# A decode attention block on one core: engines synchronized by hand, a TensorE loop, and a softmax that subtracts the maximum

## The chip, the cores and the metric

The kernel runs on one core of a Trainium2 chip. The metric is the device time of one execution in microseconds (us), the median of several runs. One profiled execution gives the trace; its page and its views are what is quoted below.

## The reference

Two sequences, one new token each (B = 2), model width D = 512. A is attention with a cache, B a small MLP block whose result gates it.

```python
xn = layernorm(x)                                  # (2, 1, 512)
# A: 32 query heads, 8 key/value heads, 32768 cached positions of width 128
q = xn @ wq                                        # (2, 32 heads, 1, 128)
scores = einsum(q, k) * 128 ** -0.5                # k, v: (2, 8, 32768, 128), each for 4 heads
s = (softmax(scores) @ v).reshape(2, 1, 4096) @ wo
# B: the shifted part is zero for a sequence of length 1
h2 = gelu(layernorm(xn) @ w3) @ w4
out = x + s * silu(xn + h2)
```

Nearly all the data is the cache: 16 pairs of K and V (2 sequences x 8 heads), each K and each V 32768 x 128 in bf16, 8.39 MB.

## The kernel before

The kernel is written against a tile framework, which allocates buffers from pools and puts in every semaphore. The work on the 16 head groups is written out, so each engine's program is one straight line.

Two rings in SBUF hold the cache: `kbuf` with three slots of 4.19 MB, `vbuf` with two. A K or V of one group takes two slots. Each partition holds 256 positions; a slot is one half of them (KPT = 128). All large loads are issued on SP's queue, in program order (lines 86, 95, 101, 114, 115, 392).

For each group `m`:

- `emit_k` is called twice, once per half. VectorE transposes K in 32x32 blocks (line 303), eight tiles `T` of 128x1024 per half, from a pool of four. TensorE multiplies each tile by the query, four matmuls of 512 columns with weights `z` (line 311), into one PSUM bank `sc`. ScalarE takes the exponential with the row sums `rs` (line 320), without subtracting a maximum. VectorE transposes the result into `pt` (line 322).
- Between the two calls the next K is issued: its slots come free when the first half of this one is transposed.
- `emit_v` is called for both halves. The row sums are added up over partitions with a matmul (line 339, `S`), and 32 matmuls per half multiply `pt` with V into the bank `o` (line 343). At the end `o` is copied (line 352), gathered (`oT`, line 355), divided by the sum (lines 360, 362) and spread (lines 365 to 372) into `oX`.
- After that the next V is issued: `vbuf` is free when the last of these matmuls is done.

Ahead of the groups stand the layernorms, the queries (line 215), and the MLP `emit_mlp`, whose weights lie in `vbuf`. Eight small loads of `x` and `xn` go through GpSimd (lines 109, 188). At the last group but one, `wo` is loaded behind the last V, in three parts, into the slot that is free by then; behind the last group 128 matmuls multiply `oX` with it (line 400), and two VectorE steps and two small stores make the output.

Of the kernel before, what the change touches and what calls it, by code (L numbers as in the profile page):

```python
# [9 lines left out]
BF16 = mybir.dt.bfloat16  # L10
ACT = mybir.ActivationFunctionType
ALU = mybir.AluOpType
AX = mybir.AxisListType

I32 = mybir.dt.int32

KPT = 128
# [4 lines left out]
EPS = 1e-5  # L22


@with_exitstack
def kernel(
# [35 lines left out]
    QP = 32 * (NQ - 1) + B  # L62

    pers = ctx.enter_context(tc.tile_pool(name="pers", bufs=1))
    rings = ctx.enter_context(tc.tile_pool(name="rings", bufs=1))
    ktp = ctx.enter_context(tc.tile_pool(name="ktp", bufs=T_BUFS))
    epp = ctx.enter_context(tc.tile_pool(name="epp", bufs=2))
    ptp = ctx.enter_context(tc.tile_pool(name="ptp", bufs=3))
    obp = ctx.enter_context(tc.tile_pool(name="obp", bufs=2))
    smp = ctx.enter_context(tc.tile_pool(name="smp", bufs=4))  # L70
    pro_ps = ctx.enter_context(tc.tile_pool(name="pro_ps", bufs=1, space=bass.MemoryType.PSUM))
    f_ps = ctx.enter_context(tc.tile_pool(name="f_ps", bufs=3, space=bass.MemoryType.PSUM))
    sc_ps = ctx.enter_context(tc.tile_pool(name="sc_ps", bufs=2, space=bass.MemoryType.PSUM))
    o_ps = ctx.enter_context(tc.tile_pool(name="o_ps", bufs=2, space=bass.MemoryType.PSUM))

    kbuf = rings.tile([128, 3 * SLOT], BF16, name="kbuf")
    vbuf = rings.tile([128, 2 * SLOT], BF16, name="vbuf")

    def row_view(cache, b, g):
        return cache[b, g, :, :].rearrange("(p t) d -> p (t d)", p=128)  # L80

    def load_k(b, g, base, parts=1):
        w = NPART * SLOT // parts
        src = row_view(A_k_cache, b, g)
        for c in range(parts):
            nc.sync.dma_start(
                out=kbuf[:, base * SLOT + c * w:base * SLOT + (c + 1) * w],
                in_=src[:, c * w:(c + 1) * w],
            )

    def load_v(b, g, parts=1):
        w = NPART * SLOT // parts
        src = row_view(A_v_cache, b, g)
        for c in range(parts):
            nc.sync.dma_start(out=vbuf[:, c * w:(c + 1) * w], in_=src[:, c * w:(c + 1) * w])  # L95


    x_bf = pers.tile([B, D], BF16)
    nc.scalar.dma_start(out=x_bf[:, :], in_=A_x[:, 0, :])
    wq_t = kbuf[:, 2 * SLOT:3 * SLOT]  # L100
    nc.sync.dma_start(  # L101
        out=wq_t[:, 0:DK * HD],
        in_=A_wq.rearrange("(p k) f -> p (k f)", k=DK),
    )

    x4_bf = pers.tile([128, QW], BF16)
    nc.gpsimd.memset(x4_bf[:, :], 0.0)
    for n in range(NQ):
        nc.gpsimd.dma_start(out=x4_bf[32 * n:32 * n + B, :], in_=A_x[:, 0, n * QW:(n + 1) * QW])
    groups = [(b, g) for b in range(B) for g in range(Hkv)]  # L110
    NG = len(groups)
    w34 = vbuf[:, 0:SLOT]
    W4O = DK * Fdim
    nc.sync.dma_start(out=w34[:, 0:W4O], in_=B_w3.rearrange("(p k) f -> p (k f)", k=DK))  # L114
    nc.sync.dma_start(out=w34[:, W4O:W4O + FK * D], in_=B_w4.rearrange("(p f) d -> p (f d)", f=FK))  # L115
    load_k(*groups[0], 0)


    ident = pers.tile([128, 128], BF16)
    make_identity(nc, ident[:, :])  # L120
    ones_f = pers.tile([128, 128], F32)
    nc.gpsimd.memset(ones_f[:, :], 1.0)


    sel = pers.tile([128, NB, 2, 4, 32], BF16)
    for j in range(4):
        nc.vector.tensor_copy(
            out=sel[:, :, :, j, :],
            in_=ident[:, :].rearrange("p (b w e) -> p b e w", b=NB, e=2),
        )  # L130

    sel_o = pers.tile([128, VT, rep], F32)
    nc.vector.tensor_reduce(
        out=sel_o[:, :, :],
        in_=ident[:, :].rearrange("p (j a t h) -> p a t h j", j=4, t=VT, h=rep)[:, 0, :, :, :],
        axis=AX.X, op=ALU.add,
    )
    sel_h = pers.tile([128, rep], F32)
    nc.vector.tensor_reduce(
        out=sel_h[:, :],  # L140
        in_=ident[:, :].rearrange("p (r h) -> p h r", h=rep),
        axis=AX.X, op=ALU.add,
    )

    sel_r = pers.tile([128, NQ, 4, 32], BF16)
    for j in range(4):
        nc.vector.tensor_copy(
            out=sel_r[:, :, j, :],
            in_=ident[:, :].rearrange("p (w r) -> p r w", r=NQ),
        )  # L150

    mask = pers.tile([128, NQ, rep], F32)
    for r in range(NQ):
        nc.vector.tensor_reduce(
            out=mask[:, r, :],
            in_=ident[:, :].rearrange("p (h w) -> p h w", h=rep),
            axis=AX.X, op=ALU.add,
        )

    zs = [pers.tile([128, NB, 2, ZC], BF16, name=f"z{i}") for i in range(2)]  # L160
    for z in zs:
        nc.gpsimd.memset(z[:, :, :, :], 0.0)


    xf = pers.tile([B, D], F32)
    nc.vector.tensor_copy(out=xf[:, :], in_=x_bf[:, :])

    def layernorm(dst, src, t):
        stats = pers.tile([B, nc.vector.BN_STATS_DIM], F32, name=f"stats_{t}")
        nc.vector.bn_stats(out=stats[:, :], in_=src[:, :])  # L170
        mv = pers.tile([B, nc.vector.BN_AGGR_DIM], F32, name=f"mv_{t}")
        nc.vector.bn_aggr(out=mv[:, :], in_=stats[:, :])
        rstd = pers.tile([B, 1], F32, name=f"rstd_{t}")
        nc.vector.tensor_scalar_add(out=rstd[:, :], in0=mv[:, 1:2], scalar1=EPS)
        nc.scalar.activation(out=rstd[:, :], in_=rstd[:, :], func=ACT.Sqrt)
        nc.vector.reciprocal(out=rstd[:, :], in_=rstd[:, :])
        nc.vector.tensor_scalar(
            out=dst[:, :], in0=src[:, :],
            scalar1=mv[:, 0:1], scalar2=rstd[:, 0:1],
            op0=ALU.subtract, op1=ALU.mult,  # L180
        )

    xn = pers.tile([B, D], F32)
    layernorm(xn, xf, "ln1")
    xn4 = pers.tile([128, QW], F32)
    nc.gpsimd.memset(xn4[:, :], 0.0)
    for n in range(NQ):
        nc.gpsimd.dma_start(out=xn4[32 * n:32 * n + B, :], in_=xn[:, n * QW:(n + 1) * QW])
    ln2 = pers.tile([B, D], F32)
    layernorm(ln2, xn, "ln2")  # L190
    xn_bf = pers.tile([B, D], BF16)
    nc.vector.tensor_copy(out=xn_bf[:, :], in_=xn[:, :])
    ln2_bf = pers.tile([B, D], BF16)
    nc.vector.tensor_copy(out=ln2_bf[:, :], in_=ln2[:, :])

    treg = pro_ps.tile([128, 2 * DK * B], BF16, tag="pro")
    for s, src in enumerate((xn_bf, ln2_bf)):
        for k in range(DK):
            c = (s * DK + k) * B
            nc.tensor.transpose(out=treg[:, c:c + B], in_=src[0:B, k::DK], identity=ident[0:B, 0:B])  # L200
    xT = pers.tile([128, 2 * DK, B], BF16)
    nc.vector.tensor_copy(out=xT[:, :, :], in_=treg[:, :].rearrange("p (k b) -> p k b", b=B))

    q_sb = pers.tile([128, B, Hq], BF16)

    oX = pers.tile([128, Hkv, NQ, B], BF16)
    g4 = pers.tile([128, QW], F32)
    x4 = pers.tile([128, QW], F32)
    nc.gpsimd.tensor_copy(out=x4[:, :], in_=x4_bf[:, :])

    wq3 = wq_t[:, 0:DK * HD].rearrange("p (k f) -> p k f", k=DK)
    qT_ps = pro_ps.tile([128, Hq * B], F32, tag="pro")
    for h in range(Hq):
        for k in range(DK):
            nc.tensor.matmul(  # L215
                qT_ps[:, h * B:(h + 1) * B],
                lhsT=wq3[:, k, h * Dh:(h + 1) * Dh],
                rhs=xT[:, k, :],
                start=(k == 0), stop=(k == DK - 1),
            )  # L220
    nc.vector.tensor_copy(out=q_sb[:, :, :], in_=qT_ps[:, :].rearrange("p (h b) -> p b h", b=B))

    qr_ps = pro_ps.tile([128, NB, 2, B * Hq], F32, tag="pro")
    for nb in range(NB):
        for e in range(2):
            nc.tensor.matmul(
                qr_ps[:, nb, e, :],
                lhsT=sel[:, nb, e, :, :].rearrange("p j w -> p (j w)"),
                rhs=q_sb[:, :, :].rearrange("p b h -> p (b h)"),
                start=True, stop=True,  # L230
            )
    qr = pers.tile([128, NB, 2, B, Hq], BF16)
    nc.vector.tensor_copy(  # L233
        out=qr[:, :, :, :, :].rearrange("p n e b h -> p (n e b h)"),
        in_=qr_ps[:, :, :, :].rearrange("p n e c -> p (n e c)"),
    )

# [54 lines left out]
    def emit_k(m, h, first):  # L292
        b, g = groups[m]
        if first:
            state["z"] = emit_z(b, g)
# [150 lines left out]
```

## Time and profile before

| what | value |
|---|---|
| time, median of 3 runs | 660.84 us (660.67 to 661.22) |
| span of the profiled execution, first to last instruction | 658.9 us |
| what lies around the span, median less span | 1.9 us |
| bytes read from HBM | 280.50 MB, 426 GB/s over the span |
| busy: PE, PEld, DVE, ACT, POOL | 386.7, 172.1, 346.0, 50.3, 6.9 us |
| mean granted TensorE clock | 0.825 |
| transposes of K, line 303 | 256, 1205 ns each |
| score matmuls, line 311 | 992 recorded, 421 ns each |

The profiled execution has no time of its own listed beside the timed runs; its span is compared with their median. PE is TensorE's matmuls, PEld its weight loads, DVE VectorE, ACT ScalarE, POOL GpSimd; SPq is SP's queue of transfers. "Landing" is the moment at which all parts of a transfer have been signalled. In the list of DMA queues the columns are packets, MB, and the share of the 16 DMA engines' time. The trace also holds every single DMA packet with its start, duration, size and queue.

### The profile page before, as it was taken

The numbers are of one execution on the slowest core, as the hardware profiler recorded it, in microseconds if no ns is written. First come the engines' busy times: TensorE is split into PE (matmuls) and PEld (weight loads), VectorE is DVE, ScalarE is ACT, GpSimd is POOL, SyncE is SP. The second block draws the span as 40 slices with busy tenths as digits, with TensorE's granted clock in tenths as the row PEclk, the third lists the DMA queues.
The fourth block names the chain that finished last, engine by engine and source line by source line (L and its number), as shares of the span: only waits on it lengthen the run. The fifth ranks groups of instructions, "written<-read, shape, count | busy, mean of one in ns | idle before, by whom it ended". The sixth has DMA issues, their size and how long they took to land.

```text
span 658.9 us, 6323 instructions
## 1 busy us (share of the span) xinstructions
PE 386.7 (59%) x2652; PEld 172.1 (26%) x2684; DVE 346.0 (53%) x442; ACT 50.3 (8%) x152; POOL 6.9 (1%) x20
## 2 busy tenths in 40 slices
PE   2338194673828557283764729377482946738764
PEld 2313132231313223131331313123131322313322
DVE  5147192754809265381935629183572918447560
ACT  1301001010100101000010100101010010100000
POOL 4000000000000000000000000000000000000000
PEclk9999688786968968697886959878596877859896
DMA  9999999999999999999999999999999999999995
GB/s 367 451 426 442 435 446 439 410 443 426 439 438 435 430 435 422 447 434 423 442 427 442 438 419 434 443 434 443 414 423 446 443 442 443 410 427 428 431 421 224
DMA packets 6704, 280.91 MB, mean 426 GB/s; under 512 B 906, under 2 KB 916, under 8 KB 1940
## 3 DMA queue, kind: packets, MB, share of 16 engines
q1 hardware_dynamic: 6408, 280.50, 98.6%
q8 instruction: 21, 0.34, 0.2%
q0 software_dynamic: 256, 0.01, 0.0%
q14 instruction: 7, 0.06, 0.0%
q10 hardware_dynamic: 12, 0.00, 0.0%
HBM read 280.50 MB, written 0.00 MB: 426 GB/s over the span
## 4 chain that ended last, share of the span: by engine, by line
DMA 75%; DVE 14%; issue 7%; PE 3%; SPq 0%; ACT 0%; DVEq 0%
DMA kbuf<-in_A_k_cache_dram 69%; DVE T L303 14%; DMA kbuf<-in_A_wo_dram 6%; PE sc L311 2%; PE o L343 1%; PE s_ps L400 0%; ACT ep L320 0%; SPq L95 0%; DVE pt L322 0%; SPq L115 0%; SPq L392 0%; SPq L114 0%; SPq L101 0%; PE S L339 0%; DVE sg L408 0%
## 5 line engine op out<-in xcount | busy, mean ns | idle before, releaser
L311 PE MATMUL sc<-T,z 128*128 128x512 bf16 x992 | 276.4, 421 | 206.3 <-DVE T L303 197.8
L303 DVE STREAM_TRANSPOSE T<-kbuf 128x1024 int32<-128x1024 int32 x256 | 291.5, 1205 | 150.5 <-DMA kbuf<-in_A_k_cache_dram 150.5
L311 PEld LDWEIGHTS <-z 128*128 128x128 bf16 x1024 | 105.7, 103 | 371.2 <-issue 278.7
L343 PE MATMUL o<-vbuf,pt 128*16 128x512 bf16 x1024 | 69.9, 434 | 3.2 <-DMA vbuf<-in_A_v_cache_dram 3.2
L320 ACT ACTIVATE ep<-sc 128x512 bf16<-128x512 f32 x32 | 19.1, 597 | 493.2 <-PE sc L311 451.2
L334 DVE MEMSET o<- 128x512 f32 x16 | 7.8, 485 | 69.3 <-ACT ob L352 68.3
L322 DVE STREAM_TRANSPOSE pt<-ep 128x512 bf16<-128x512 bf16 x32 | 22.6, 707 | 34.7 <-ACT ep L320 34.4
L343 PEld LDWEIGHTS <-pt 128*16 128x16 bf16 x1024 | 27.2, 99 | 37.9 <-issue 18.2
L339 PE MATMUL S<-sm,ones_f 128*128 128x4 f32 x64 | 10.7, 238 | 26.1 <-DVE sm L338 26.1
L355 PE MATMUL oT<-sel_o,ob 128*128 128x4 f32 x128 | 16.9, 255 | 11.1 <-ACT ob L352 11.1
L355 PEld LDWEIGHTS oT<-sel_o,ob 128*128 128x128 f32 x128 | 15.5, 191 | 19.3 <-ACT ob L352 19.3
L339 PEld LDWEIGHTS S<-sm,ones_f 128*128 128x128 f32 x64 | 10.7, 188 | 30.9 <-DVE sm L338 28.4
L352 ACT COPY ob<-o 128x512 f32<-128x512 f32 x16 | 9.4, 586 | 83.4 <-PE o L343 83.4
L362 DVE TENSOR_TENSOR on<-oT,rec 128x4 bf16<-128x4 f32 x16 | 2.6, 162 | 21.8 <-PE oT L355 21.8
L286 ACT COPY z<-qr 32x16 bf16<-32x16 bf16 x64 | 12.6, 198 | 11.5 <-DVE qr L233 10.9
L360 DVE RECIPROCAL rec<-S 128x4 f32<-128x4 f32 x16 | 2.9, 182 | 7.6 <-PE S L339 7.6
L365 PEld LDWEIGHTS <-sel_r 128*128 128x128 bf16 x64 | 5.2, 117 | 5.2 <-issue 5.2
L320 ACT ACTIVATION_READ_ACCUMULATOR ep<-sc 128x1 f32 x32 | 6.3, 198 | 0.2
L215 PE MATMUL qT_ps<-xT,kbuf 128*128 128x2 bf16 x128 | 3.6, 165 | 4.5 <-DMA kbuf<-in_A_wq_dram 4.5
L365 PE MATMUL xp<-on,sel_r 128*128 128x4 bf16 x64 | 3.8, 164 | 4.1 <-DVE on L362 4.1
L338 DVE TENSOR_SCALAR sm<-sel_h,rs 128x4 f32<-128x4 f32 x32 | 6.0, 188 | 0.0
L370 DVE TENSOR_TENSOR xm<-xp,mask 128x16 f32<-128x16 f32 x16 | 2.8, 174 | 5.3 <-PE xp L365 5.3
(64 smaller groups left out, 48.5 us busy)
## 6 DMA issues: line engine op xcount, KB each, us to landing
kbuf<-in_A_k_cache_dram SPq DMA_DIRECT2D x2, 4096.0 KB, 29.1
vbuf<-in_A_v_cache_dram SPq DMA_DIRECT2D x2, 4096.0 KB, 26.7
kbuf<-in_A_wq_dram SPq DMA_DIRECT2D x1, 4096.0 KB
vbuf<-in_B_w_dram SPq DMA_DIRECT2D x2, 1792.0 KB, 21.6
kbuf<-in_A_wo_dram SPq DMA_DIRECT2D x1, 2048.0 KB, 35.9
kbuf<-in_A_wo_dram SPq DMA_DIRECT2D x1, 1536.0 KB, 39.1
kbuf<-in_A_wo_dram SPq DMA_DIRECT2D x1, 512.0 KB
kbuf<-in_A_k_cache_dram SPq DMA_DIRECT2D x15, 29.4
```

Source lines behind the costliest of these rows:

```text
L286: nc.scalar.copy(out=z[32 * j:32 * j + 32, :, :, c:c + rep], in_=qr[32 * j:32 * j + 32, :, :, b, g * rep:(g + 1) * rep],)
L303: nc.vector.transpose(out=T[:, :].rearrange("p (b t k) -> p t b k", b=NB, t=RT), in_=kt[:, r * W:(r + 1) * W].rearrange("p (t b k) -> p t ...
L311: nc.tensor.matmul(sc[:, :], lhsT=z[:, nb, e, zc:zc + 128], rhs=Tb[:, nb, :, e], start=(r == 0 and nb == 0 and e == 0), stop=(r == NR - 1 ...
L320: nc.scalar.activation(out=ep[:, :], in_=sc[:, :], func=ACT.Exp, scale=inv_sqrt_dh, accum_out=rs[:, :])
L322: nc.vector.transpose(out=pt[:, :, :].rearrange("p r (t h) -> p t r h", h=rep), in_=ep[:, :].rearrange("p (t r h) -> p t r h", r=NR, h=rep),)
L334: nc.vector.memset(state["o"][:, :], 0.0)
L338: nc.vector.tensor_scalar_mul(out=sm[:, :], in0=sel_h[:, :], scalar1=rs[:, 0:1])
L339: nc.tensor.matmul(S[:, :], lhsT=ones_f[:, :], rhs=sm[:, :], start=(i == 0), stop=(i == NPART - 1))
L343: nc.tensor.matmul(o[32 * j:32 * j + VT * rep, :], lhsT=pt[:, r, a * VT * rep:(a + 1) * VT * rep], rhs=vt[:, u * VT:(u + 1) * VT, :].rearr ...
L352: nc.scalar.copy(out=ob[:, :], in_=o[:, :])
L355: nc.tensor.matmul(oT[:, :], lhsT=ob[:, t * Dh:(t + 1) * Dh], rhs=sel_o[:, t, :], start=(t == 0), stop=(t == VT - 1),)
L365: nc.tensor.matmul(xp[:, r, :], lhsT=sel_r[:, r, :, :].rearrange("p j w -> p (j w)"), rhs=on[:, :], start=True, stop=True,)
```

## The change

The computation is written in one section in which the framework puts in no semaphores. A small class `Queue` wraps each engine, counts the instructions that signal, and attaches the waits that are named by hand. Buffers are allocated once, by name.

- TensorE's work on a group is the body of a loop of 16 passes, whose first instruction lies at the start of a block of 256 instructions (`head_slot`). Its waits are on semaphores that it counts down again (`take`). The other engines' programs stay written out.
- The scores keep two banks; both exponentials of a group wait for the head's maximum over all positions: VectorE reduces each half (`peak`), a matmul with `same_h` spreads the row maxima, VectorE reduces again, and ScalarE subtracts the result in the exponential. `z` is one buffer instead of two, filled for the next group behind the exponentials.
- The next K now waits for the matmuls of the eighth tile (`s_T`) and not for its transpose; the next V waits for the last V matmul as before (`s_X`).
- The first half in `order(m)` no longer decides which V half comes first: it is always half 0.
- `o` is cleared once, not once per group. The MLP's second product is 14 matmuls of 512 columns instead of 56 of 128. The four small loads of `x` and four that spread the gate are issued on ScalarE's queue; GpSimd issues none.
- TensorE's built program shrinks from 344,320 to 65,152 bytes (64 bytes an instruction; the loop body has 317 instructions), VectorE's from 42,496 to 35,840.

The core of the changed side:

```diff
+    with tc.tile_critical(no_gpsimd_drain=True):
...
+        for n in range(NQ):
+            ac.op(lambda e, n=n: e.dma_start(out=x4_bf[32 * n:32 * n + B, :], in_=A_x[:, 0, n * QW:(n + 1) * QW]), e_x4z, inc=(d_x4, 16))
...
+        load_v(0, e_h2)
+        for m in range(1, NG):
+            half = (s_T, NT * (m - 1) + NR)
+            base = m % 2
+            if m < NG - 1:
+                sp.op(lambda e, m=m, base=base: e.dma_start(
+                    out=kbuf[:, base * SLOT:(base + NPART) * SLOT], in_=row_view(A_k_cache, *groups[m])),
+                    half, e_q, inc=(d_k[0], 16))
...
+            load_v(m, (s_X, NX * (m - 1) + 3))
...
+            def peak(i):
+                e = ve.op(lambda v: v.tensor_reduce(out=mx[:, i:i + 1], in_=sc[i][:, :], axis=AX.X, op=ALU.max), (s_T, m * NT + (i + 1) * NR))
+                ve.op(lambda v: v.tensor_scalar_mul(out=mxr[:, i, :], in0=row_of[:, :], scalar1=mx[:, i:i + 1]), e,
+                      inc=(t_mx, 1) if i == NPART - 1 else False)
+            for i, h in enumerate((first, second)):
...
+                for r in range(NR):
...
+                    ve.op(lambda v, n=n, r=r, kt=kt: v.transpose(
...
+                        landed(h), used, inc=(t_T, 1))
+                    if i == 1 and r == 3:
+                        peak(0)
+            peak(1)
+            e = ve.op(lambda v: v.tensor_reduce(out=top[:, :], in_=S[:, rep:], axis=AX.X, op=ALU.max), (s_X, NX * m + 1))
+            e = ve.op(lambda v: v.tensor_scalar_mul(out=shift[:, :], in0=top[:, :], scalar1=-inv_sqrt_dh), e)
+            e_exp = [ac.op(lambda v, i=i: v.activation(
+                out=ep[i][:, :], in_=sc[i][:, :], func=ACT.Exp, scale=inv_sqrt_dh, bias=shift[:, :], accum_out=rs[i][:, :]),
+                e, e_tf if m == 0 else None) for i in range(NPART)]
...
+        def take(s, n=1):
+            nc.tensor.wait_ge(s, n).then_inc(s, -n)
+        with nc.Fori(0, NG, engines=[PE], head_slot={PE: 0}):
+            take(t_z)
+            for i in range(NPART):
+                for r in range(NR):
+                    take(t_T)
...
+                    ins.then_inc(s_T, 1)
+            take(t_mx)
+            nc.tensor.matmul(
+                S[:, rep:], lhsT=same_h[:, :], rhs=mxr[:, :, :].rearrange("p i r -> p (i r)"),
+                start=True, stop=True).then_inc(s_X, 1)
+            take(t_pt, NPART)
...
+            for h in range(NPART):
+                take(t_v[h], 16)
...
```

## The prediction

> **What bounds the kernel now.** I read the page first: the slices, the DMA queues, the chain.
>
> ```profile
> DMA  9999999999999999999999999999999999999995
> ...
> q1 hardware_dynamic: 6408, 280.50, 98.6%
> q8 instruction: 21, 0.34, 0.2%
> q0 software_dynamic: 256, 0.01, 0.0%
> q14 instruction: 7, 0.06, 0.0%
> ...
> DMA 75%; DVE 14%; issue 7%; PE 3%; SPq 0%; ACT 0%; DVEq 0%
> ```
>
> The 16 DMA engines are busy in every slice but the last, and 280.5 MB of the 280.9 MB are the loads on SP's queue. The chain names DVE for 14%, so I checked whether a compute wait ever lets that queue run dry: the windows view between landings of K (columns: length; PE, PEld, DVE, ACT, POOL busy; clock, DMA share, GB/s).
>
> ```profile
> 197.22:235.82 38.60, 22.79 (x142) 9.90 (x144) 20.97 (x26) 2.76 (x9) 0.00 (x0) 0.81 1.00 432
> 235.82:275.61 39.79, 24.13 (x142) 10.28 (x144) 20.95 (x26) 2.76 (x9) 0.00 (x0) 0.80 1.00 432
> ```
>
> One head group takes 38.6 us, the DMA share is 1.00, and DVE is busy for 21 us of it. So DVE's 14% is only the path over which the next load is issued; the transfer then waits behind others anyway. Timeline of one group:
>
> ```profile
> 244.97 0.33 SPq L86 DMA_DIRECT2D kbuf<-in_A_k_cache_dram  x1
> ...
> 263.09 0.33 SPq L95 DMA_DIRECT2D vbuf<-in_A_v_cache_dram  x1
> ...
> 275.61 11.39 DVE L303 STREAM_TRANSPOSE T<-kbuf 128x1024 int32<-128x1024 int32 x10 [9.91 <-DMA kbuf<-in_A_k_cache_dram]
> ```
>
> With K landed at 235.8, the next K is issued 9.2 us later and the next V 27.3 us later. The first transfer of the kernel began 1.0 us after its issue (0.74 to 1.76). V of this group ends half a period, 19.3 us, after K, and the next K after 38.6. Spare time is thus 19.3 - 9.2 - 1.0 = 9.1 us for K and 38.6 - 27.3 - 1.0 = 10.3 us for V.
>
> **What sets the length of the stream.** The trace's single DMA packets tell the rest. A 65,536 B packet of K or V takes 2.418 us, and each DMA engine runs its packets back to back, so they can be strung into 16 chains. All carry the same bytes, yet they end apart: seven at 649.2 to 649.7 us, four at 652.0 to 652.2, five at 653.5 to 653.7. The difference is code. The 21 packets of q8 have 16,384 B each, 344,064 B together, and TensorE's built program has 344,320 B: they are its instructions, one packet per block as it goes. They go round over eight engines: before the stream ends four engines serve three and four serve two. A code packet takes 0.88 to 0.97 us and the data packet after it 2.9 us, some 0.5 over the usual, so 1.43 us each; (653.57 - 649.2) / 3 gives 1.45. VectorE's program (42,496 B) comes in 8,192 B packets, five of q14, all on one further engine, which ends at 653.69: (653.69 - 649.2) / 5 = 0.89 us each. Two code packets in one period (243.1 and 268.9) also explain the 39.79 us window. The kernel ends thus:
>
> ```profile
> 652.79 1.88 PE L400 MATMUL s_ps<-kbuf,oX 128*2 128x128 bf16 x64 [2.00 <-DMA kbuf<-in_A_wo_dram]
> 654.71 0.29 DVE L408 TENSOR_TENSOR sg<-s_ps,g 98x128 f32<-98x128 f32 x1 [4.53 <-PE s_ps L400]
> ```
>
> The last sixteen of these matmuls start at 654.03, when the slowest engine's part of wo (653.69) has been signalled. So: end = slowest DMA engine + 5.2 us.
>
> **The change part by part.**
>
> *TensorE's loop.* The program shrinks from 5,380 to 1,018 instructions (65,152 B); the body is 317 instructions, 20,288 B, from the start of a block: one whole block and 61 slots of the next. The trace of before has no backward branch. Lower bound: the body stays on the chip after its first pass; TensorE then fetches about four blocks, one on each of four engines, which end at 649.2 + 1.44 = 650.6. Upper bound: all that a pass touches is fetched again, two blocks and the one ahead: 3 x 16 and some three more, 51 over eight engines, seven on the worst, 649.2 + 7 x 1.44 = 659.3. I take the lower end: in before every block came once and just ahead of use, with no PE wait put down to it, and the body is under two of these blocks. A stall at the branch itself costs nothing at once: TensorE has about 10 us without work before each K (225.5 to 235.8), 7 of them left after the longer chain below. [...]
>
> *VectorE's code.* 35,840 B instead of 42,496: 4.4 packets of 8,192 B instead of 5.2. Before, five were fetched, coming when its program stood at instructions 61 to 71 modulo 128; in 560 instructions that makes four. Its engine ends at 649.2 + 4 x 0.89 = 652.8 and is now the slowest: -0.9 us (0 with five, -1.8 with three). This caps what the loop can gain: four TensorE engines would be done at 650.6, but wo waits for all sixteen.
>
> *The maximum.* Per group DVE gains two reductions over 128x512, two small products, one small reduction and one product, and loses the memset of o (0.485). No row has that reduction; 128x512 rows of DVE go from 0.485 (memset) to 0.707 (transpose): 0.65, close to the transpose, since it also reads every element. Both exps now stand behind both score halves. From the landing of K: 16 transposes at 1.138 = 18.2; first maximum and product 0.85, 19.05; last four matmuls 1.15 (transposes' end 254.66 to the exp at 255.81), 20.2; second maximum and product with gaps 0.9, 21.1; the matmul that spreads it 0.4 (the 0.39 of S), 21.5; two small DVE steps 0.45, 21.95; two exps at 0.60 + 0.20, 23.55; sum and transpose 0.19 + 0.71 and gaps, 24.6; S 0.39, 25.0; 64 matmuls 5.32, 30.3; issue of V at 30.7, against 27.3. All of these 3.4 us lie under V's 10.3: 6.9 remain. K now waits for the eighth tile's matmuls rather than its transpose: 10.6 (the first exp starts 10.5 us after the landing) against 9.2; 7.7 remain. Cost on the end: 0. If reductions cost twice the longest row, 1.4 each, V still has 5.4 us. DVE rises from 21 to about 23 of 38.6 us.
>
> *Last group.* K's second half has landed at about 625 and is transposed by 634.5; by the same steps V's matmuls start at 640.6 and the first 32 end by 642.5 to 644.0; the last V part lands at 644.15 as before. Nothing is later, and wo has four more us of cover.
>
> *Order of the small steps.* Four x loads move from POOL to ACT ahead of its first Sqrt: 4 x 0.55 us (the x_bf issue), so the layernorm starts some 1.2 us later; wq lands at 13.3, xT stood ready at 10.7, and V0 is issued near 28 instead of 25, against K0's 42.3. The MLP's 14 wide matmuls for 56 narrow ones: 3 to 6 us for 1.7, under the same cover. g4's four loads on ACT come 16 groups before their use.
>
> *GpSimd loads.* 256 packets of mostly 9 ns: 2.3 us over 16 engines, -0.15.
>
> *Entry and exit of the section.* One more signal and branch before SP's first issue at 0.74: a semaphore step of SP takes 0.07 us in the last rows, two to three give +0.2 (0 to 0.3). At the end SP passes ten waits from 656.15 to 658.12; now it is one for the output and six for engines: 0 (-0.4 to +0.4).
>
> Sum against the span of 658.9: -0.9 - 0.15 + 0.2 + 0 = -0.85, 658.1. The timed runs' median lies 1.9 us over the span (660.84), and nothing here touches that part: 660.0.
>
> **Rivals.**
>
> *The loop is fetched again in each pass.* Once past the block's end, the block ahead may take the place of the loop's head. For it: code came in single blocks, one ahead, as if no more were held. Against: nothing in the trace shows a block twice, since no code ran twice. Three per pass: 659.3 against 653.69, +5.6, with the other terms 666.5; two per pass (35 fetches, five on the worst engine, 656.4): +2.7, 663.6. From the third fetch per engine on, it decides. Slower. 25%. [...]
>
> *One fetch per pass.* Only the second block comes anew: about 20 fetches, three on the worst engine, 653.6, as before: with the other terms 660.8. 10%.
>
> *The same block always from the same engine.* The rotation of before also fits a fixed place for each block. If so and if each pass fetches, one engine serves 16 more: 649.2 + 17 x 1.44 = 673.7, about 681. 6%.
>
> *V is issued too late.* If the longer chain took 6.9 us more than worked out, each further us would come 15 times. PE's 5 us pause ahead of V could cost some clock (granted 0.81 here), but 64 matmuls at half speed add 5.3 at most. An excess of 0.3 to 1 us makes 660 + 15 x 0.3 to 1, 665 to 675. 5%.
>
> *A larger gain.* VectorE's code in three packets (-1.8), the exit 0.4 shorter, the entry free, or several of these: 658.5 to 659.5. 18%.
>
> **How the numbers follow.** Forecast, loop kept and four VectorE packets: 36%, own range 659.5 to 660.7. A measurement of this kernel tells 0.2%, 1.3 us, from no change. Faster by more: the larger gain, 0.18. Same: forecast and one fetch per pass, 0.46. Slower: the rest, 0.36. The range leaves out the lowest 7% or so and the two far rivals: 659.0 to 667.0.
>
> **What would show it.** q8 with four to six packets rather than 21, q14 with one fewer; groups of 38.6 us with DMA share 1.00; V issued 30 to 32 us after K's landing; the last wo landing near 652.8. Wrong if q8 carries 30 packets or more, if a group takes over 39 us, or if PE waits at the loop's head after K has landed.

## The result, and the profile after

The changed kernel takes 663.0 us (median of seven runs, 661.89 to 665.56) against 660.84: a ratio of 1.0041, with an interval of 1.0027 to 1.0055. It is slower by 2.2 us, where the forecast had it 0.85 us faster. Its profiled execution has a span of 661.0 us against 658.9.

The page of the changed kernel: the queues (packets, MB, share of 16 engines), the chain that ended last, and the group of the new reductions.

```profile
q1 hardware_dynamic: 6408, 280.50, 98.4%
q8 instruction: 4, 0.07, 0.0%
q14 instruction: 5, 0.04, 0.0%
...
PE 0%; DVE 0%; issue 0%
PE pro L479 0%; DVE sg L412 0%; DVE out L413 0%; PE xp L466 0%
...
L373 DVE TENSOR_REDUCE mx<-sc 128x1 f32<-128x512 f32 x32 | 21.5, 671 | 20.0 <-PE sc L432 20.0
```

The loads are the same 280.5 MB. TensorE's code has shrunk to four packets from 21, VectorE's to four (the fifth of q14 is ScalarE's). The chain view breaks off after a few steps, but it names what ended last: no longer a DMA of `wo`, as the 128 matmuls of line 479 now follow on VectorE and PE alone.

One group in the timeline (start, length, engine, line, operation; in brackets the idle time and its releaser):

```profile
236.55 13.63 DVE L383 STREAM_TRANSPOSE T<-kbuf 128x1024 int32<-128x1024 int32 x12 [4.61 <-DMA kbuf<-in_A_k_cache_dram]
...
246.97 0.33 SPq L337 DMA_DIRECT2D kbuf<-in_A_k_cache_dram  x1
...
267.21 0.33 SPq L325 DMA_DIRECT2D vbuf<-in_A_v_cache_dram  x1
```

From K's landing at 236.55 the next K is issued after 10.4 us and the next V after 30.7, so nothing in the group comes too late for the queue. And yet a group is longer. The windows of this group and of the last two, each from one start of line 383 to the next and then to the first `wo` matmul (length; PE, PEld, DVE, ACT, POOL; clock, DMA share, GB/s):

```profile
236.55:275.25 38.70, 24.55 (x144) 9.81 (x146) 22.55 (x30) 2.72 (x9) 0.00 (x0) 0.85 1.00 434
586.87:621.05 34.18, 25.51 (x144) 10.50 (x146) 22.47 (x30) 2.71 (x9) 0.00 (x0) 0.81 0.99 429
621.05:655.01 33.96, 25.50 (x144) 10.26 (x147) 22.30 (x30) 2.03 (x5) 0.00 (x0) 0.85 0.89 373
```

Two things differ from the prediction. First, the group takes 38.70 us and not 38.60, at a DMA share of 1.00. Second, the last group starts 34.18 us after the one ahead of it, where before it was 28.95 (586.15 to 615.10). The end of the timeline shows why:

```profile
618.37 0.80 SPq L330 DMA_DIRECT2D vbuf<-in_A_v_cache_dram  x2
...
620.97 0.17 DVE L408 TENSOR_REDUCE oX<-xm 128x4 bf16<-128x16 f32 x1
621.05 13.62 DVE L383 STREAM_TRANSPOSE T<-kbuf 128x1024 int32<-128x1024 int32 x12
...
646.76 5.71 PE L451 MATMUL o<-vbuf,pt 128*16 128x512 bf16 x64
...
655.01 1.96 PE L479 MATMUL pro<-kbuf,oX 128*2 128x128 bf16 x128
...
657.02 0.29 DVE L412 TENSOR_TENSOR sg<-pro,g 98x128 f32<-98x128 f32 x1 [1.73 <-PE pro L479]
...
657.67 0.66 SPq L415 DMA_DIRECT2D out_dram<-out  x1
```

The first transpose of the last group has no bracket: it waits for no transfer. Its K had been signalled in full at 615.92 us, 5.1 us before. In VectorE's program it stands behind `oX`, the last small step of group 14, and it starts 0.08 us after that step's start. The same place in the kernel before, which the prediction did not look at:

```profile
586.15 11.38 DVE L303 STREAM_TRANSPOSE T<-kbuf 128x1024 int32<-128x1024 int32 x10 [9.76 <-DMA kbuf<-in_A_k_cache_dram]
...
614.77 0.17 DVE L372 TENSOR_REDUCE oX<-xm 128x4 bf16<-128x16 f32 x1
...
615.10 1.25 DVE L303 STREAM_TRANSPOSE T<-kbuf 128x1024 int32<-128x1024 int32 x1 [0.16 <-DMA kbuf<-in_A_k_cache_dram]
```

There VectorE was done 0.16 us before K landed. That is all the slack the group had.

With the end of the stream (the last packet of `wo`, from the trace's single packets) at 654.72 us instead of 653.68 and the step `sg` 2.3 us behind it instead of 1.0, both halves of the loss are in sight: the stream ends late, although it carries less code, and the computation then ends late behind the stream.

### The profile page after: what moved, and what is told of

Its sections match the earlier page's. It is cut to its first block, busy times and chain, and to the rows that moved or that the text cites. A ratio compares the mean times of both kernels' runs of the same rounds, so it can differ in the third digit from the quotient of the medians.

```text
span 661.0 us, 6555 instructions
## 1 busy us (share of the span) xinstructions
PE 422.7 (64%) x2642; PEld 176.3 (27%) x2674; DVE 373.2 (56%) x526; ACT 50.0 (8%) x152; POOL 1.7 (0%) x10
## 5 line engine op out<-in xcount | busy, mean ns | idle before, releaser
L432 PEld LDWEIGHTS sc<-T,z 128*128 128x128 bf16 x1024 | 97.8, 103 | 304.9 <-issue 227.4
L451 PE MATMUL o<-vbuf,pt 128*16 128x512 bf16 x1024 | 92.8, 542 | 0.0
L392 ACT ACTIVATE ep<-sc,shift 128x512 bf16<-128x512 f32 x32 | 21.7, 683 | 461.2 <-DVE shift L391 461.2
L451 PEld LDWEIGHTS o<-vbuf,pt 128*16 128x16 bf16 x1024 | 31.0, 119 | 54.0 <-issue 47.4
L443 PE MATMUL S<-sm,ones_f 128*128 128x4 f32 x64 | 14.6, 333 | 48.2 <-PEq L420 48.2
L373 DVE TENSOR_REDUCE mx<-sc 128x1 f32<-128x512 f32 x32 | 21.5, 671 | 20.0 <-PE sc L432 20.0
L438 PE MATMUL S<-mxr,same_h 128*128 128x64 f32 x32 | 6.5, 285 | 18.4 <-PEq L420 18.4
L438 PEld LDWEIGHTS S<-mxr,same_h 128*128 128x128 f32 x32 | 4.8, 188 | 26.2 <-issue 26.2
L390 DVE TENSOR_REDUCE top<-S 128x1 f32<-128x64 f32 x16 | 3.6, 225 | 9.4 <-PE S L438 9.4
L374 DVE TENSOR_SCALAR mxr<-row_of,mx 128x32 f32<-128x32 f32 x32 | 7.7, 242 | 1.1
## 6 DMA issues: line engine op xcount, KB each, us to landing
kbuf<-in_A_k_cache_dram SPq DMA_DIRECT2D x15, 28.1
```

Of the source, the lines that this page charges most:

```text
L373: e = ve.op(lambda v: v.tensor_reduce(out=mx[:, i:i + 1], in_=sc[i][:, :], axis=AX.X, op=ALU.max), (s_T, m * NT + (i + 1) * NR))
L374: ve.op(lambda v: v.tensor_scalar_mul(out=mxr[:, i, :], in0=row_of[:, :], scalar1=mx[:, i:i + 1]), e, inc=(t_mx, 1) if i == NPART - 1 else ...
L392: e_exp = [ac.op(lambda v, i=i: v.activation(out=ep[i][:, :], in_=sc[i][:, :], func=ACT.Exp, scale=inv_sqrt_dh, bias=shift[:, :], accum_ou ...
L432: ins = nc.tensor.matmul(sc[i][:, :], lhsT=z[:, nb, w, zc:zc + 128], rhs=Tb[:, nb, :, w], start=(r == 0 and nb == 0 and w == 0), stop=(r = ...
L438: nc.tensor.matmul(S[:, rep:], lhsT=same_h[:, :], rhs=mxr[:, :, :].rearrange("p i r -> p (i r)"), start=True, stop=True).then_inc(s_X, 1)
L443: ins = nc.tensor.matmul(S[:, 0:rep], lhsT=ones_f[:, :], rhs=sm[i][:, :], start=(i == 0), stop=(i == NPART - 1))
```

## The experiments

Twelve runs, each timed in five rounds beside the kernel before, which took 660.87, 660.85 and 660.80 us in the three sets. "End of the stream" is the last packet of `wo` in the profiled execution.

**Without the maximum.** The exponentials go back to waiting for their own scores; the two reductions over a score half, the small reduction and the spreading matmul go. The kernel leaves out the subtraction.

```diff
-                    if i == 1 and r == 3:
-                        peak(0)
-            peak(1)
-            e = ve.op(lambda v: v.tensor_reduce(out=top[:, :], in_=S[:, rep:], ...), (s_X, NX * m + 1))
-            e = ve.op(lambda v: v.tensor_scalar_mul(out=shift[:, :], ...), e)
...
-                out=ep[i][:, :], ..., bias=shift[:, :], accum_out=rs[i][:, :]),
-                e, ...
+                out=ep[i][:, :], ..., accum_out=rs[i][:, :]),
+                (s_T, m * NT + (i + 1) * NR), ...
```

> The changed kernel without the maximum: both reductions, the matmul that spreads it and the shift are gone, each exponential waits for its own scores alone (the softmax is then the one of before, without the subtraction). Theory (the tail): after K of group 14 has landed no transfer is waited for; the chains of groups 14 and 15 run one behind the other, 34.2 + 34 us, and end at 655, after the last wo (652.6). Without the maximum each chain is about 3.4 us shorter, the end falls back to the stream: VectorE's first output step at 653.6 instead of 657.0, span 657.6, time 659.5. Rival (the stream): the longer chain or the slower packets (2.422 us for 2.418) delay the transfers themselves; then the wo landing is what counts and the time stays at 662 to 663.

Measured: 661.77 us (661.4 to 661.91), ratio 1.0013 (1.0004 to 1.0022). The last group starts at 615.44 again and `sg` comes 1.3 us behind the stream, nearly as soon as before (1.0), so 1.2 us belong to the maximum. But the theory of the tail alone fell short: 1 us over the kernel before stays, where it should have been over 1 us below. The stream ends at 654.55.

**The last two groups alone.** In groups 14 and 15 the exponentials do not wait for the maximum (they run without a shift, and a memset stands where the first reduction was); groups 0 to 13 keep it.

```diff
+                        if m < NG - 2:
                             peak(0)
+                        else:
+                            ve.op(lambda v: v.memset(mxr[:, :, :], 0.0), ..., inc=(t_mx, 1))
```

> The changed kernel, but in groups 14 and 15 alone the exponentials do not wait for the maximum and none is subtracted there (TensorE's loop stays the same; its spread matmul runs on zeros). Theory (the tail): only the last two groups' chains count, so the time falls as without the maximum at all, to 659.5 to 660. Rival (the stream): fourteen groups still have the longer chain, so 662.5 to 663.

Measured: 661.78 us (661.61 to 661.92), the same as without any maximum, and like it some 2 us above what the theory named. In fourteen groups the longer chain costs nothing; its 1.2 us come from the last two.

**Four transposes ahead.** Group 15's first four transposes are put ahead of group 14's small steps on VectorE.

```diff
+            if m == NG - 2:
+                kl = kbuf[:, SLOT:2 * SLOT].bitcast(I32)
+                for r in range(T_BUFS):
+                    put_T((NG - 1) * NT + r, r, kl, (d_k[0], 16 * NG))
```

> The changed kernel, maximum kept; the first four transposes of group 15 stand ahead of group 14's last small steps on VectorE (its K half landed some 5 us before). Theory (the tail): VectorE no longer starts group 15 only after group 14's end (621.05); four tiles are ready for TensorE when it comes back, and group 15's scores end about 2.0 us sooner, paced by TensorE at 1.13 us a tile: time 661.0 instead of 663.0. Rival (the stream): nothing in the transfers changes, 663.

Measured: 661.81 us (661.42 to 664.11), ratio 1.0022 (1.0013 to 1.0031). The maximum's cost is hidden, by its median and its profile (stream's end 654.29, last matmul 655.19), and again 1 us stays.

**The maximum in the kernel before.** The same reductions, products and matmul, written for the framework.

> The kernel before with the maximum alone put in (same reductions, matmul and shift; both exponentials behind it), unrolled and synchronized by the framework as before. Theory (the tail): the chains of the last two groups grow by 3.4 us and more each, group 15 starts at 619 to 621 instead of 615.1, and the end moves from the last wo (653.7) to about 656: time 662 to 663.5. Rival (the stream): 10 us of cover for each load, so 660.9 to 661.2.

Measured: 663.27 us (663.03 to 664.27), ratio 1.0043 (1.0029 to 1.0056): as slow as the whole change, more than the maximum should cost, and the stream ended at 656.24, 2.6 us late. TensorE's code comes in 21 packets, as before, and VectorE's in one more (seven on the queue before, eight here):

```profile
q14 instruction: 8, 0.07, 0.0%
```

One of VectorE's packets came at 653.55 us, while parts of `wo` were still to come. It took 0.33 us, and two 4,096 B packets of `wo` after it took 0.50 and 0.49 us instead of 0.16. From 655.3 us on, one DMA engine alone is still busy with `wo`. So some 0.9 of the 2.6 us are code, and 1.6 to 1.7 us are left. Nothing in the added work issues or delays a transfer in the middle groups, which leaves the packets themselves. In the kernel before, 98% of the 65,536 B packets of K and V take 2.418 us. In the changed kernel and in all four experiments so far their median is 2.420 to 2.422, and the slowest twentieth takes 2.426 or more. What these five have in common is the place of the buffers. `kbuf` and `vbuf` started at bytes 36352 and 134656 of each partition; in the changed kernel they start at 16512 and 114816, and in the last experiment at 36992 and 135296, because small buffers ahead of them were dropped or added. The first pair are multiples of 256; the other two pairs lie 128 past one. Three of the next four runs, and two later ones, ask for the place.

**The changed kernel with its buffers moved.** 384 B more ahead of `kbuf`: 16896 and 115200.

```diff
+    sb("pad", [128, 96], F32)
```

> The changed kernel with an unused tile of 384 bytes a partition ahead of the rings, nothing else. In the changed kernel kbuf begins at SBUF byte 16512 and vbuf at 114816 of each partition, both 128 past a multiple of 512; in the kernel before both lie on a multiple (36352, 134656). Theory (place): the K and V packets of the changed kernel take 2.422 us instead of 2.418 because of that place; with the tile they take 2.418, the groups 38.60 us instead of 38.70, K of group 14 is transposed from 585.4 instead of 586.9, and since the chain of the last two groups starts there the time falls by 1.5: 661.5. Rival (activity): packets are slower because of what the engines do beside them; 38.70 and 663.0 stay.

Measured: 660.30 us, ratio 1.0005 (0.9993 to 1.0017): 2.7 us less for a buffer that nobody reads, and 1.2 us less than the theory named. The packets take 2.418 us again, the stream ends at 652.84, and a group is back at 38.60 (windows view, columns as above):

```profile
313.88:352.48 38.60, 24.89 (x146) 9.83 (x146) 22.54 (x31) 2.71 (x9) 0.00 (x0) 0.85 1.00 435
```

Eight of the twelve runs lie between 659.75 and 660.76, four between 662.69 and 663.83.

**The same without the maximum.**

> The changed kernel without the maximum (the exponential subtracts nothing, as before) and with the 384 byte tile. Theory (place): the stream is the limit without the maximum (661.77, last wo at 654.55), and loses 0.1 us in each of 16 groups and as much in V, wo and wq: last wo at 652.8, as worked out in the prediction, time 660.1. Rival (activity): 661.8.

Measured: 659.82 us (659.51 to 660.09), ratio 0.9983 (0.9974 to 0.9992). This is the fastest kernel of the study. The timeline of its end:

```profile
613.88 0.17 DVE L404 TENSOR_REDUCE oX<-xm 128x4 bf16<-128x16 f32 x1
613.97 18.22 DVE L384 STREAM_TRANSPOSE T<-kbuf 128x1024 int32<-128x1024 int32 x16
...
649.39 1.39 PE L471 MATMUL pro<-kbuf,oX 128*2 128x128 bf16 x64
...
652.00 1.88 PE L471 MATMUL pro<-kbuf,oX 128*2 128x128 bf16 x64 [1.21 <-DMA kbuf<-in_A_wo_dram]
...
653.92 0.29 DVE L408 TENSOR_TENSOR sg<-pro,g 98x128 f32<-98x128 f32 x1 [4.26 <-PE pro L471]
```

Half of the `wo` matmuls are done and the rest wait for a transfer, as in the kernel before. The stream ends at 652.79 us, and the prediction's time for its end was 652.8.

**The kernel before with its buffers moved.** 128 B ahead of the rings: 36480 and 134784. Nothing else differs.

```diff
+    rings.tile([128, 32], F32, name="pad")
```

> The kernel before with an unused tile of 128 bytes a partition ahead of the rings: kbuf at 36480, vbuf at 134784, 128 past a multiple of 512; nothing else. Theory (place): packets 2.422, groups 38.70, time 660.87 + 1.6 = 662.4. Rival (activity): 660.9.

Measured: 662.63 us (662.57 to 662.71), ratio 1.0026 (1.0017 to 1.0036), 1.78 us slower, with the stream's end at 655.33. Two groups in the windows view:

```profile
158.71:197.40 38.69, 23.47 (x144) 9.95 (x144) 20.96 (x25) 2.76 (x9) 0.00 (x0) 0.81 1.01 434
508.92:547.62 38.70, 24.45 (x144) 10.06 (x144) 20.85 (x26) 2.76 (x9) 0.00 (x0) 0.81 1.00 432
```

The computation of these groups is that of before (DVE 20.9 us, PE 23 to 24), and still they take 0.10 us more. So a busier VectorE or PE is not needed for the loss.

The tile also moves everything behind the rings, `T` among it, by the same 128 B, and no run moves the rings alone. The packets speak against these other buffers as the cause: between 100 and 580 us, the 599 packets during which no engine computes have a median of 2.422 us, the same as the 1,297 beside a VectorE busy for over 90% of the packet. But the place does not lengthen every packet from the start. Of those that begin between 25 and 39 us, before the first K has landed, 88 of 94 take 2.418 us; between 100 and 200 us it is 150 of 662. What makes them longer later is not shown.

**The loop written out**, without the maximum, with the buffers at the changed kernel's place.

```diff
-        with nc.Fori(0, NG, engines=[PE], head_slot={PE: 0}):
+        for _ in range(NG):
```

> The changed kernel without the maximum and with TensorE's loop written out (python for): against the run without the maximum alone (661.77) only the loop differs. Theory (code): some 20 code packets of TensorE come back, three on the slowest engines: 3 x 1.44 = 4.3 us of lag instead of VectorE's 4 x 0.89 = 3.6, so the last wo lands 0.7 later and the time is 662.4 to 662.8. Rival (the branch costs): if entering the loop anew cost the stream something, 661.5 or less.

Measured: 662.56 us (662.44 to 663.32), 0.79 more than the first experiment, of which it is a copy with that one edit. The page has

```profile
q8 instruction: 22, 0.36, 0.2%
```

and the stream ends at 655.33 instead of 654.55, 0.78 later. So the loop is worth 0.8 us, and through its code packets.

**Moved by 256 B.** The kernel before with 256 B ahead of the rings: 36608 and 134912, multiples of 256 but not of 512.

```diff
+    rings.tile([128, 64], F32, name="pad")
```

> The kernel before with an unused tile of 256 bytes: kbuf at 36608, vbuf at 134912, 256 past a multiple of 512. If any place off a multiple of 512 costs the same: 662.6, as with 128 bytes. If 256 is enough: 660.9.

Measured: 660.77 us (660.53 to 661.04), ratio 0.9999. In the windows view

```profile
119.62:158.22 38.60, 24.14 (x142) 10.31 (x144) 20.96 (x25) 2.76 (x9) 0.00 (x0) 0.81 1.01 435
```

the group is at 38.60. Here a multiple of 256 is enough, and the loss is not one of moving the buffers as such.

**The maximum in the kernel before, with its buffers moved**, by 384 B to 37376 and 135680.

> The kernel before with the maximum, its rings moved by a 384 byte tile so that both start on a multiple of 512 bytes again (37376, 135680). Without the tile, at 128 past a multiple, it took 663.27. Theory (place and tail): the place was worth 1.78 there (the kernel before with a 128 byte tile against itself), the rest is the maximum's chain in the last groups: 661.5. Rival (the maximum costs it all): 663.3.

Measured: 661.71 us (661.23 to 662.63), ratio 1.0015 (1.0006 to 1.0024); 1.56 less than without the 384 B. The stream ends at 653.56, as in the kernel before. What is left of the maximum is 0.9 us by the medians. The profiled execution is one of four long ones (662.59 to 662.63; the other seven are at 661.23 to 661.72): in it the last group starts at 620.04, and the last matmul stands at 656.36, 2.8 us behind the stream.

**Buffers moved and four transposes ahead**, in the changed kernel with its maximum.

> The changed kernel, maximum kept, with the 384 byte tile and with the first four transposes of group 15 ahead of group 14's last small steps. With the tile alone it took 660.30 (659.75 to 663.83): last wo at 652.84, but the last matmul at 654.5 against 653.56 without the maximum, so the last two chains still set the end by 1 us and more in some runs. Theory (place and tail): with the four transposes moved up the end falls to the stream, 659.8 as without the maximum, and the runs lie closer together. Rival (place alone): the tail has no more part in it, 660.3.

Measured: 660.58 us (659.4 to 662.9), ratio 1.0003 (0.9992 to 1.0014). In its timeline the last group starts behind K's landing again, and `sg` comes 1.0 us behind the stream's end (652.87):

```profile
614.27 4.62 DVE L354 STREAM_TRANSPOSE T<-kbuf 128x1024 int32<-128x1024 int32 x4 [4.33 <-DMA kbuf<-in_A_k_cache_dram]
...
651.87 1.96 PE L488 MATMUL pro<-kbuf,oX 128*2 128x128 bf16 x128
...
653.88 0.29 DVE L421 TENSOR_TENSOR sg<-pro,g 98x128 f32<-98x128 f32 x1 [1.73 <-PE pro L488]
```

Its profile, of an execution of 659.87 us, is that of a kernel without the cost, but the median cannot be told from that of the moved buffers alone (660.30), and the runs lie no closer together. Whether the move of the transposes helps is not settled.

**The loop's head moved within a block.** The fastest kernel, with the loop's head at slot 200 of a block of 256 instructions. The run was meant to spread the body over three blocks. But its 312 instructions are 56 in one block and 256 in the next, so by this count it still lies on two.

```diff
-        with nc.Fori(0, NG, engines=[PE], head_slot={PE: 0}):
+        with nc.Fori(0, NG, engines=[PE], head_slot={PE: 200}):
```

> The changed kernel without the maximum and with the 384 byte tile, and the head of TensorE's loop moved from slot 0 to slot 200 of a block: the 312 instructions of the body then lie on three blocks of 256 instead of two. Theory (the body stays on the chip whatever its place): four or five code packets of TensorE and 659.8, as with slot 0. [...]

Measured: 659.99 us (659.57 to 661.02), not to be told from 659.82, and

```profile
q8 instruction: 4, 0.07, 0.0%
```

No pass fetched the body again, with its head at slot 0 or at slot 200. A body on three blocks was not tested; the changed kernel's body covers two.

## Why the prediction was wrong

**What held.** *TensorE's loop*: four packets, one per block, and none between 74.25 us and 656.96, behind the last pass; a loop that is fetched again would have brought 35 or 51, and the rivals that rest on one fell with it. With the head at slot 200 there are four as well. *VectorE's code*: four packets, and its engine sets the end at 652.8; measured 652.79, 652.84, 652.87 and 652.93 in the four kernels with four packets of VectorE's code and the buffers at multiples of 256. *The maximum* in a group: 671 ns a reduction (0.65 taken), K issued 10.4 us after the landing (10.6), V 30.7 (30.7), DVE busy for 22.55 us (about 23), and no cost in fourteen groups. *Order of the small steps*: V0 issued at 28.1 us (near 28). *Entry*: the first packet at 1.99 instead of 1.76 us, +0.23 (+0.2). *Exit*: 3.3 us from the issue of the last store to the end of the span instead of 3.5, within its bounds. With the buffers moved and without the maximum the kernel takes 659.82, and the forecast was 660.0.

**What was missing: the place of the buffers.** The sum took a K or V packet at 2.418 us, as in before, and had no term for where it lands. The change allocates every buffer anew by name, and `kbuf` and `vbuf` ended up 128 B past a multiple of 256. It costs 1.78 us in the kernel before (moved by 128 B), 1.95 in the changed kernel without its maximum (661.77 less 659.82) and 1.56 in the kernel before with it (where VectorE's late packet has a part in the number). Over 16 groups, 0.10 us each make 1.6. The packets explain about half of that: 256 packets of 65,536 B in a group over 16 engines are 16 on each, at 3.5 ns more some 0.06 us. I did not break down the rest. A packet measured 0.14% more and a group 0.26%. With 256 B instead of 128 there was no cost (660.77 us, a group at 38.60). What makes a packet longer at such a place is not shown, nor why the packets of the first K were hardly longer (88 of 94 at 2.418 us).

**What was wrong: "Last group", and in it "Nothing is later".** The prediction followed K's second half and the last V from their landing, and put the last group's V matmuls at 640.6 us; they started at 646.76 (at 644.73 with the buffers moved). It forgot that VectorE has to be free. So the sum's 0 for the maximum was wrong. In group 14 the chain behind K is longer by the maximum, its last gathering step starts at 620.97 instead of 614.77, and only behind it does VectorE take up a K that, in before, it began at 615.10 on landing. The cover of ten us that the middle groups have is time until a transfer begins; behind the last V there is no transfer to wait for, and the slack there was the 0.16 us of the bracket above. The 34.18 us between the two starts are one chain: transposes, maximum, exponentials, V matmuls, gathering. The `wo` matmuls then start at 655.01, with the last packet of `wo` in at 654.72, and wait for none of it. The cost is 1.2 us in the changed kernel (663.0 against 661.77), 0.9 in the kernel before and 0.5 in the one with the buffers moved; how much shows depends on where the stream ends.

**The account**, against the predicted end of the stream: -0.85 as predicted, +1.8 to 1.95 for the place, +1.2 for the tail make 2.15 to 2.3; measured 2.16. In the profiled execution: 658.05 us predicted; the stream ended 1.87 after 652.85; `sg` came 2.3 behind it instead of 1.03, +1.27; the steps from `sg` on took 0.25 less: 660.9, and the span is 661.0.

**What stays open.** The kernels with the maximum scatter: 661.89 to 665.56 us for the changed one, 659.75 to 663.83 with moved buffers, 659.4 to 662.9 with the transposes ahead as well. Of those without it, the first experiment lies within 0.5 us and the fastest kernel within 0.6, the written-out loop within 0.9, and the kernel with the moved head within 1.5 by one run. The kernel that drops the maximum in the last two groups alone lies within 0.3, so the scatter goes with the last two chains. With moved buffers the four long runs have mean granted clocks of 0.803 to 0.808 and the others 0.808 to 0.821, which would fit a last chain that runs on PE at a lower clock; but the changed kernel has 662.24 us at 0.798, and the one with transposes ahead 659.82 at 0.804 and 661.25 at 0.813. No run isolates it. So moving the buffers took 2.7 us off the changed kernel, more than the 1.95 of its version without the maximum, and I cannot say how much of the difference is scatter. Places of 32 or 64 B past a multiple, and `kbuf` and `vbuf` moved one at a time, were not tried.

## What to carry to other kernels

Where a stream of transfers sets the length, a change that only reallocates buffers can cost more than it gains (1.6 to 1.95 us of 660 here): look up the start of every large transfer's destination, before and after, and put it on a multiple of 256 B. Spare time worked out in the steady state can end with the last transfers (here ten us became 0.16); follow the last groups separately, engine by engine in program order, and read the smallest bracket there as the slack. Code is a load too: string the packets of each DMA engine and see which engine ends last, since here that one, not the sum, decided what less code was worth (18 packets fewer for TensorE gave 0.8 us, because VectorE's four stayed).

## What the runs showed of the hardware

With destinations 128 B past a multiple of 256, the packets of 65,536 B had a median of 2.420 to 2.422 us instead of 2.418, and a group's 16.8 MB took 38.70 us instead of 38.60; 256 B past a multiple of 512 cost nothing (38.60). The packets of the first K were hardly longer (88 of 94 at 2.418). TensorE's loop of 312 to 317 instructions ran 16 passes from four code packets in all, with its head at slot 0 and at slot 200. A code packet of 8,192 B near the end of the stream took 0.33 us, and two data packets of 4,096 B after it 0.50 and 0.49 us instead of 0.16; the stream's end came 0.9 us later.
